# A linear attention with a mixture of experts on one core: the second expert's weights are split in other places, its loads stand behind other rows, and a few small steps around the hand-over change their order

## The chip, the cores and the metric

The kernel runs as one program on one core of a Trainium2 chip. The metric is the device time of the whole program in microseconds (us), as a median of runs; lower is better. The engines are named as in the profile: PE is the matmul engine, DVE the vector engine, ACT the scalar engine, POOL the general-purpose engine, and SP the engine that here only issues transfers (SPq, POOLq and so on are the engines' queues of such instructions). Each engine works through its own instructions in the order in which they were written down, and waits at an instruction until what it needs is there.

## The reference

The inputs are r, k, v, w of shape (4, 8, 768, 48), u (8, 48), a gate (384, 8), and for each of 8 experts w1 (384, 1024) and w2 (1024, 384).

```python
for t in range(S):                                   # attention with a decaying state, per batch and head
    cur = einsum('bhd,bhe->bhde', u * k[t], v[t])
    y[t] = einsum('bhd,bhde->bhe', r[t], state + cur)
    state = w[t][..., None] * state + einsum('bhd,bhe->bhde', k[t], v[t])
x = y as (3072, 384)                                 # 3072 tokens
expert = argmax(x @ w_gate); gate = softmax(x @ w_gate)[expert]
for e in range(8):                                   # each token goes through its one expert
    xe = x[expert == e]
    out[expert == e] = gate * (relu(xe @ w1[e]) @ w2[e])
```

## The kernel before

**First phase.** The attention runs over 24 blocks of 128 tokens; `iteration(n)` issues the stages of several blocks beside each other. After the blocks of a chunk of the sequence are done, a gate decides each token's expert, `rank` (PE) and `place` (DVE) give it a row in that expert's list, and `scatter` (a POOL transfer with computed addresses, line 674) writes the token into `xs` in memory. The last chunk is handled in four groups, `each[0]` to `each[3]`; `chosen(i)` does place, weight and scatter of group i. `gate(...)`, `count(...)` and `act_ex(...)` are the steps ahead of `rank`.

**Second phase.** Every matrix product is done in three matmuls over a high and a low half of each operand (xh, xl; w1h, w1l; w2h, w2l; hh, hl). A weight piece comes from memory (`load_piece`, SP, tiles `wst` and `wsp`) and is split into halves by `split_piece`: ACT writes the high half (line 228), DVE the low one (line 230). An expert has four pieces, i = 0, 1 of w1 and 2, 3 of w2, each split in three parts. There are two sets of split weights, `wts[0]` and `wts[1]`. `stg[e, i]` is the loaded, unsplit piece i of expert e. The eight experts are taken in an order by their number of tokens; the first two are chosen before the attention ends, the other six by `sort_experts` on DVE, followed by `check`.

**Where the phases meet.** The first expert's rows are worked on while the attention ends, in two parts: `pa` (2 x 128 rows) and `pb` (2 x 104 rows). A part loads its rows (`load_rows`, line 248, SP), turns them (`trans`: PE transposes `pt` at line 284, ACT line 285, DVE line 286), and goes through `mm1(f)` for f = 0 to 7 (PE `bank` line 293, then ACT `hh` line 295 and DVE `hl` line 296) and `mm2(q)` (PE `opt` line 310, DVE `ort` line 315, POOL scatter of the result). An `mm2` is 24 matmuls over f = 0 to 7; a dictionary {f: [...]} names what is issued behind its step f. `split_more()` issues the next part of the first expert's own weights. Behind the two parts comes the loop over the other seven experts: `expert(e)` reads the expert's number on SP (line 691), `load_x` its rows, `trans_x` turns them, `feed(e, i)` splits a piece and asks for the next one from memory (`feed(e, i, False)` only asks).

**What sets the order.** Inside `tc.manual_schedule(...)` the engines named there keep the order of the code. SP is not among them, and neither is any engine in the loop over experts: there a scheduler orders, and it may also draw instructions of the loop up between those of the code ahead of it. SP's transfers are issued one after the other, so one that waits holds up those behind it. The pool `wpb` with the second weight set takes the memory of pools that are closed just ahead of it (among them `sm`), so the first writer into the second set waits for the last reader of the tiles that lay there.

Of the kernel before, what the change touches and what calls it, by code (L numbers as in the profile page):

```python
# [8 lines left out]
F32 = mybir.dt.float32  # L9
# [46 lines left out]
def rwkv_moe_kernel(ctx, tc, rkw, vv, ub, wgp, wg, w1, w2, wc, out):  # L56
# [536 lines left out]
            ch["pi", c, b + i] = pi[:, i:i + 1]  # L593

    def sort_keys(k, out):
        ks = sm.tile([1, E], F32, name="ks", tag="ks")
        nc.vector.max(out=ks, in_=k)
        ki = sm.tile([1, E], I32, name="ki", tag="ki")
        nc.vector.tensor_copy(ki, ks)
        nc.vector.tensor_single_scalar(out=out, in_=ki, scalar=E - 1, op=ALU.bitwise_and)  # L600
        return ks
# [15 lines left out]

    def sort_experts():
        cn = counts()
        ch["all"] = sm.tile([1, 1], F32, name="all", tag="all", bufs=1)  # L620
        nc.vector.tensor_reduce(out=ch["all"], in_=cn[0:1, :], axis=AX.X, op=ALU.add)
        c0 = sm.tile([1, NST, E], F32, name="c0", tag="c0", bufs=1)
        nc.vector.tensor_tensor(out=c0, in0=cn[0:1, :].unsqueeze(1).broadcast_to([1, NST, E]), in1=first_e, op=ALU.mult)
        ch["c0"] = sm.tile([1, NST], F32, name="c1", tag="c1", bufs=1)
        nc.vector.tensor_reduce(out=ch["c0"], in_=c0, axis=AX.X, op=ALU.add)
        for i in range(NST):
            nc.vector.scalar_tensor_tensor(out=key, in0=first_e[:, i, :], scalar=-65536.0, in1=key, op0=ALU.mult, op1=ALU.add)
        ch["ks"] = sort_keys(key, order)
# [30 lines left out]
        nc.vector.tensor_copy(flag, lo[:, 4:5])  # L659

    def check():
        bad = sm.tile([1, E + 2 + NST], F32, name="bad", tag="bad", bufs=1)
        nc.vector.tensor_single_scalar(out=bad[:, E:E + 1], in_=ch["all"], scalar=float(NTOK), op=ALU.not_equal)
        nc.vector.tensor_tensor(out=bad[:, 0:E], in0=ch["ks"], in1=capk, op=ALU.is_ge)
        nc.vector.tensor_tensor(out=bad[:, E + 2:E + 2 + NST], in0=ch["c0"], in1=capc, op=ALU.is_gt)
        lo = sm.tile([1, E], F32, name="lo", tag="lo", bufs=1)
        nc.vector.tensor_single_scalar(out=lo[:, 0:E - NST], in_=ch["ks"][:, 0:E - NST], scalar=float(LEAST * E), op=ALU.is_lt)
        nc.vector.tensor_single_scalar(out=lo[:, E - NST:E], in_=ch["c0"], scalar=LEAST - 0.5, op=ALU.is_lt)
        nc.vector.tensor_reduce(out=bad[:, E + 1:E + 2], in_=lo, axis=AX.X, op=ALU.max)
        nc.vector.tensor_reduce(out=any_, in_=bad, axis=AX.X, op=ALU.max)  # L670
# [65 lines left out]
    def iteration(n):  # L736
# [73 lines left out]
        if n == ROUTED:  # L810
# [3 lines left out]
            for i in range(3):  # L814
                wsl.append(wst.tile([P, NT], F32, name="wst", tag="wst"))
                stg[0, i] = load_piece(eid[0], i, wsl[i])
        if n == 19:
            stg[1, 0] = load_piece(eid[1], 0, spare())


    wts = [wt0]
# [124 lines left out]
    with tc.manual_schedule(engines={ET.PE, ET.DVE, ET.Activation, ET.Pool}):  # L946
        for n in range(-3, NB - 2):
            iteration(n)
            if n == 21:
                split_more()  # L950
                stg[1, 2] = load_piece(eid[1], 2, spare())
            if n == 20:
                pa = Part(0, HA // 2, ld.tile([P, NT], F32, name="xg0", tag="rkwt"))
                pa.split_tiles()
                full, banks = banks, banks[0:2]
                stg[1, 1] = load_piece(eid[1], 1, spare())

        lc, n2, n3 = NCH - 1, NB - 2, NB - 1
# [8 lines left out]
        pe_a(n2)  # L967
        dve_at(n2)
        dve_kh(n3)
        stg[1, 3] = load_piece(eid[1], 3, spare())  # L970
        pool_diag(n3)
        act_diag(n3, slice(0, 3))
        pe_lp(n2 - 1)
# [48 lines left out]
        pe_pick(n3)  # L1022
        act_xr(n3)
        rank(each[2])
        chosen(2)
        gate(each[3])
        count(each[3])
        act_ex(each[3])
        split_more()
        pa.mm1(2)  # L1030
        rank(each[3])
        chosen(3)
        split_more()
        pa.mm1(3)
        split_more()
        pa.mm1(4)
        split_more()
        pb = Part(HA, HB // 2, ld.tile([P, NT], F32, name="xg0", tag="rkwt"))
        for f in (5, 6, 7):
            pa.mm1(f)  # L1040
            split_more()
        pb.split_tiles()
        sort_experts()
        expert(2)
        feed(1, 0, False)
        check()
        actx.close()
        wpb = mctx.enter_context(tc.tile_pool(name="wpb", bufs=1))
        wts.append(weight_tiles(wpb))
        split_piece(wts[1], stg[1, 0], 0)  # L1050
        feed(1, 1, False)
        split_piece(wts[1], stg[1, 1], 1)
        feed(1, 2, False)
        load_x(1)
        pa.mm2(0)
        pa.mm2(1, {f: [lambda j=j: pb.trans(j)] for j, f in enumerate((0, 2, 4))})
        banks = full
        nth["b"] = 0
        for f in range(8):
            pb.mm1(f)  # L1060
            if f in (1, 3, 5):
                split_piece(wts[1], stg[1, 2], 2, part=f // 2)
        split_piece(wts[1], stg[1, 3], 3)
        pb.mm2(0, {f: [lambda j=j: trans_x(1, j)] for j, f in enumerate((2, 6))})
        pb.mm2(1, {1: [lambda: trans_x(1, 2)]})
    fin = None
    load_w(0)
    load_w(1)
    for e in range(1, E):
        if e == E - 2:  # L1070
            bad = nc.values_load(flag[0:1, 0:1], min_val=0, max_val=1)
        expert(e + 2)
        if e + 1 < E:
            load_x(e + 1)
        hs = mm1(e, fin)
        fin = mm2(e, hs)
    mctx.close()


# [198 lines left out]
```

## Time and profile before

| what | value |
| --- | --- |
| time, median of 3 runs | 385.31 us (384.91 to 386.27) |
| the profiled execution's own time | 387.93 us |
| its span, first to last instruction | 386.2 us |
| busy: PE, DVE, ACT, POOL | 95%, 71%, 53%, 35% |
| mean granted clock of PE | 0.989 |

The profiled execution has 1.73 us outside its span, and is 0.7% longer than the median. All positions below are us from the start of its span. A row of the timeline gives start, duration, engine, line, operation, output<-input, shapes and count, and in brackets the idle time of the engine just ahead with what ended it. In the rows by windows, each engine's busy time (and count of instructions) comes first, then the granted clock as a share of full speed, the share of time in which the transfer engines were busy, and GB/s.

### The profile page before, as it was taken

How to read it: one execution, taken by the hardware profiler on the slowest of the kernel's cores; microseconds unless marked ns; L12 is line 12 of the kernel's file. 1: busy time of each engine (PE TensorE's matmuls, PEld its weight loads, DVE VectorE, ACT ScalarE, POOL GpSimd, SP SyncE). 2: the span in 40 equal slices, each digit the busy share in tenths (PEclk: the TensorE clock that was granted, in tenths of full speed). 3: DMA queues.
4: the chain of work that ended last, by engine and by line, in shares of the span. 5: the costliest groups of instructions: out<-in, count | busy, mean ns of one | idle time of the engine just before them, and what ended most of it. 6: DMA issues, size and time to landing. Idle time of an engine off the chain costs nothing.

```text
span 386.2 us, 9326 instructions
## 1 busy us (share of the span) xinstructions
PE 368.3 (95%) x3522; PEld 338.5 (88%) x3522; DVE 273.6 (71%) x531; ACT 205.2 (53%) x559; POOL 134.2 (35%) x204
## 2 busy tenths in 40 slices
PE   8989999999999889799999999999999999999991
PEld 6668888888888679799999999999999999999990
DVE  4999999898999868598784792895792853622310
ACT  4989787787777656383625533633633642511200
POOL 4765588868767351102000510400320402112020
PEclk9999999999999999899999999999999999999997
DMA  8999977777518882957394465665365533001010
GB/s 285 406 338 323 308 231 227 241 230 232 164 64 305 272 285 77 282 175 242 114 306 134 145 201 185 193 211 182 98 231 174 157 123 119 21 0 58 1 40 19
DMA packets 32996, 71.44 MB, mean 185 GB/s; under 512 B 3960, under 2 KB 20235, under 8 KB 32946
## 3 DMA queue, kind: packets, MB, share of 16 engines
q1 hardware_dynamic: 29298, 61.32, 49.5%
q0 software_dynamic: 3648, 9.47, 6.8%
q8 instruction: 29, 0.48, 0.5%
q14 instruction: 21, 0.17, 0.1%
HBM read 58.94 MB, written 12.14 MB: 184 GB/s over the span
## 4 chain that ended last, share of the span: by engine, by line
PE 78%; DVE 9%; ACT 5%; issue 3%; DMA 2%; POOL 1%; SPq 1%; POOLq 0%; ACTq 0%; DVEq 0%
PE bank L293 28%; PE bank L920 14%; PE opt L310 13%; PE yp L496 4%; PE ap L484 4%; PE yp L514 3%; PE yq L521 2%; DVE at L383 2%; PE pt L284 2%; DVE pre L361 2%; PE st L505 2%; DMA rkwt<-in_rkw_dram 2%; PE kbank L475 1%; PE op L909 1%; ACT at L355 1%
## 5 line engine op out<-in xcount | busy, mean ns | idle before, releaser
L293 PE MATMUL bank<-xl,w1h 128*128 128x440 f32 (+6 forms) x168 | 58.4, 348 | 0.0
L293 PE MATMUL bank<-xh,w1l 128*128 128x440 f32 (+6 forms) x168 | 58.0, 345 | 0.0
L254 POOL DMA_INDIRECT out_dram<-ot,xg x16 | 21.3, 1332 | 103.2 <-DVE ot L910 99.5
L293 PE MATMUL bank<-xh,w1h 128*128 128x440 f32 (+6 forms) x168 | 55.5, 352 | 0.0
L355 ACT ACTIVATE at<-ident,cl 128x128 f32<-128x128 f32 x168 | 53.8, 393 | 0.0
L254 POOL DMA_INDIRECT out_dram<-ort,xg x13 | 13.0, 1004 | 94.7 <-DVE ort L315 79.6
L295 ACT ACTIVATE hh<-bank 128x256 fp32r<-128x256 f32 (+8 forms) x58 | 26.7, 470 | 34.9 <-PE bank L293 31.2
L230 DVE TENSOR_TENSOR w2l<-wst,w2h 128x512 fp32r<-128x512 f32 x42 | 27.5, 687 | 24.8 <-ACT w2h L228 21.4
L296 DVE SCALAR_TENSOR_TENSOR hl<-bank,hh 128x256 fp32r<-128x256 f32 (+8 forms) x58 | 29.9, 528 | 14.0 <-ACT hh L295 14.0
L334 POOL TENSOR_TENSOR rk<-rkwt 112x512 f32<-112x512 f32 x24 | 30.7, 1280 | 20.4 <-DMA rkwt<-in_rkw_dram 5.1
L383 DVE COPY_PREDICATED at<-cmask,ap 128x512 f32<-128x512 int32 x48 | 32.5, 731 | 2.6 <-PE ap L484 2.5
L343 POOL TENSOR_TENSOR rh<-rkwt,pre 112x512 f32<-112x512 f32 x24 | 28.9, 1205 | 12.0 <-DVE pre L361 10.8
L361 DVE TENSOR_TENSOR_SCAN pre<-rkwt,st 112x533 f32<-112x533 f32 x24 | 30.0, 1250 | 3.6 <-DMA rkwt<-in_rkw_dram 3.6
L293 PEld LDWEIGHTS bank<-xl,w1h 128*128 128x128 f32 x168 | 31.7, 188 | 0.5
L228 ACT ACTIVATE w2h<-wst 128x512 fp32r<-128x512 f32 x42 | 24.5, 626 | 14.2 <-PE bank L920 9.9
L293 PEld LDWEIGHTS bank<-xh,w1l 128*128 128x128 f32 x168 | 31.6, 188 | 0.5
L293 PEld LDWEIGHTS bank<-xh,w1h 128*128 128x128 f32 x168 | 31.4, 188 | 0.5
L369 DVE TENSOR_TENSOR_SCAN suf<-rkwt,st 112x533 f32<-112x533 f32 x24 | 30.3, 1264 | 0.8
L674 POOL DMA_INDIRECT xs<-xr,pi x24 | 25.3, 1053 | 14.0 <-DVE kh L377 3.8
L230 DVE TENSOR_TENSOR w1l<-wst,w1h 128x512 fp32r<-128x512 f32 x42 | 27.5, 685 | 1.0 <-ACT w1h L228 0.8
L310 PE MATMUL opt<-w2h,hh 128*128 128x384 f32 (+3 forms) x82 | 28.2, 350 | 0.0
L310 PE MATMUL opt<-w2h,hl 128*128 128x384 f32 (+3 forms) x82 | 28.0, 343 | 0.0
(164 smaller groups left out, 874.6 us busy)
## 6 DMA issues: line engine op xcount, KB each, us to landing
rkwt<-in_rkw_dram SPq DMA_DIRECT2D x23, 780.0 KB
wst<-in_w_dram SPq DMA_DIRECT2D x42, 256.0 KB
wst<-in_w_dram SPq DMA_DIRECT2D x14, 768.0 KB
vt<-in_vv_dram SPq DMA_DIRECT2D x24, 192.0 KB
wct<-in_wc_dram SPq DMA_DIRECT2D x24, 192.0 KB
xg<-xs SPq DMA_DIRECT2D x5, 579.0 KB
xs<-zrow SPq DMA_DIRECT2D x8, 289.5 KB
wsp<-in_w_dram SPq DMA_DIRECT2D x6, 256.0 KB
```

What stands on the lines that cost most here:

```text
L230: nc.vector.tensor_tensor(out=lo, in0=st[:, cs], in1=hi.bitcast(F32), op=ALU.subtract)
L254: i = nc.gpsimd.indirect_dma_start(out=out[:, :], out_offset=bass.IndirectOffsetOnAxis(ap=t.bitcast(I32)[:, q, DM + 1:DM + 2], axis=0), in ...
L293: nc.tensor.matmul(hp, a, x[:, j, :], start=(i == 0), stop=(i == 8))
L296: nc.vector.scalar_tensor_tensor(out=hl, in0=hp, scalar=0.0, in1=hh.bitcast(F32), op0=ALU.max, op1=ALU.subtract)
L310: nc.tensor.matmul(op, a[:, cs], w2v(wt, w, f), start=(i == 0), stop=(i == 23))
L334: i = nc.gpsimd.tensor_tensor(out=d["rk"], in0=d["r"], in1=d["k"], op=ALU.mult)
L343: nc.gpsimd.tensor_tensor(out=d["rh"], in0=d["r"], in1=d["pre"][:, :, 2:C + 2], op=ALU.mult)
L355: nc.scalar.activation(blk[n]["at"][:, j, q], ident, AF.Copy, scale=blk[n]["ct"][:, 2 * q + j:2 * q + j + 1])
L361: nc.vector.tensor_tensor_scan(out=pre[:, 0:NS], data0=d["w"], data1=floor(n), initial=0.0, op0=ALU.mult, op1=ALU.max)
L369: nc.vector.tensor_tensor_scan(out=suf[:, 0:NS][:, ::-1], data0=d["w"][:, ::-1], data1=floor(n), initial=0.0, op0=ALU.mult, op1=ALU.max)
L383: d["atc"] = nc.vector.copy_predicated(out=d["at"][:, j], mask=cmask.unsqueeze(1).broadcast_to([P, NP_, C]), data=d["ap"][j]).ins
L920: nc.tensor.matmul(pp, w, a, start=(i == 0), stop=(i == 23))
```

## The change

Five things change.

1. The tiles of `sort_keys`, `sort_experts` and `check` are taken from the pool `const` instead of `sm`.
2. The load of the second expert's piece 0, `stg[1, 0]`, is issued behind the rows of `pa` instead of ahead of them. Its piece 3 is issued behind the rows of `pb`, into a buffer that the first expert's piece 1 has left.
3. The gate of the fourth group stands ahead of `chosen(2)`; its `rank` and `chosen(3)` stand behind `pa.mm1(3)` instead of ahead of it.
4. The second expert's splits stood in a block of six between `check` and `pa.mm2(0)`, then three between steps of `pb.mm1`, then three ahead of `pb.mm2`. Now single parts stand at steps of `pa.mm2(0)`, `pa.mm2(1)`, `pb.mm1(1)` to `(6)`, `pb.mm2(0)` and `(1)`. `expert(2)` and the requests for the third expert's pieces stand behind `load_x(1)`, both after `pa.mm2(1)`.
5. The loop over experts is put under `manual_schedule` for POOL alone.

```diff
-        ks = sm.tile([1, E], F32, name="ks", tag="ks")
+        ks = const.tile([1, E], F32, name="ks", tag="ks", bufs=2)
...
-        bad = sm.tile([1, E + 2 + NST], F32, name="bad", tag="bad", bufs=1)
+        bad = const.tile([1, E + 2 + NST], F32, name="bad")
...
-        if n == 19:
-            stg[1, 0] = load_piece(eid[1], 0, spare())
...
                 pa = Part(0, HA // 2, ld.tile([P, NT], F32, name="xg0", tag="rkwt"))
                 pa.split_tiles()
                 full, banks = banks, banks[0:2]
+                stg[1, 0] = load_piece(eid[1], 0, spare())
                 stg[1, 1] = load_piece(eid[1], 1, spare())
...
-        stg[1, 3] = load_piece(eid[1], 3, spare())
...
         rank(each[2])
-        chosen(2)
         gate(each[3])
         count(each[3])
         act_ex(each[3])
+        chosen(2)
         split_more()
         pa.mm1(2)
+        split_more()
+        pa.mm1(3)
         rank(each[3])
         chosen(3)
-        split_more()
-        pa.mm1(3)
         split_more()
         pa.mm1(4)
         split_more()
         pb = Part(HA, HB // 2, ld.tile([P, NT], F32, name="xg0", tag="rkwt"))
+        stg[1, 3] = load_piece(eid[1], 3, wsl[1])
         for f in (5, 6, 7):
             pa.mm1(f)
             split_more()
         pb.split_tiles()
-        sort_experts()
-        expert(2)
-        feed(1, 0, False)
-        check()
         actx.close()
         wpb = mctx.enter_context(tc.tile_pool(name="wpb", bufs=1))
         wts.append(weight_tiles(wpb))
-        split_piece(wts[1], stg[1, 0], 0)
-        feed(1, 1, False)
-        split_piece(wts[1], stg[1, 1], 1)
-        feed(1, 2, False)
-        load_x(1)
-        pa.mm2(0)
-        pa.mm2(1, {f: [lambda j=j: pb.trans(j)] for j, f in enumerate((0, 2, 4))})
+        sort_experts()
+        check()
+
+        def part(i, p):
+            return lambda: split_piece(wts[1], stg[1, i], i, part=p)
+
+        pa.mm2(0, {5: [part(0, 0)]})
+        pa.mm2(1, {0: [lambda: pb.trans(0), part(0, 1)], 2: [lambda: pb.trans(1), part(0, 2)], 4: [lambda: pb.trans(2)]})
+        load_x(1)
+        expert(2)
+        feed(1, 0, False)
+        feed(1, 1, False)
         banks = full
         nth["b"] = 0
         for f in range(8):
             pb.mm1(f)
-            if f in (1, 3, 5):
-                split_piece(wts[1], stg[1, 2], 2, part=f // 2)
-        split_piece(wts[1], stg[1, 3], 3)
-        pb.mm2(0, {f: [lambda j=j: trans_x(1, j)] for j, f in enumerate((2, 6))})
-        pb.mm2(1, {1: [lambda: trans_x(1, 2)]})
+            if 0 < f < 7:
+                part(1 + (f - 1) // 3, (f - 1) % 3)()
+        pb.mm2(0, {0: [part(3, 0)], 2: [lambda: trans_x(1, 0)], 4: [part(3, 1)], 6: [lambda: trans_x(1, 1)]})
+        pb.mm2(1, {1: [lambda: trans_x(1, 2)], 3: [part(3, 2)]})
+        feed(1, 2, False)
...
-    for e in range(1, E):
+    with tc.manual_schedule(engines={ET.Pool}):
+        for e in range(1, E):
```

On DVE, between the sort and the turned rows of `pb`, the kernel before has these instructions in this order (`w1l<-wsp` is a split of the second expert's w1, `x_2835` the turned rows of `pb`, `hhl` and `hl` results of `pb.mm1`):

```order
L670 TENSOR_REDUCE any<-bad 1x1
L230 TENSOR_TENSOR w1l<-wsp,w1h 128x512 x6
L300 TENSOR_SCALAR xg_2357<-xg_2357 128x2
L301 RECIPROCAL xg_2357<-xg_2357 128x2
L315 TENSOR_SCALAR ort<-opt,xg_2357 128x384
L286 TENSOR_TENSOR x_2835<-pt,x_2835 128x208 x3
L315 TENSOR_SCALAR ort<-opt,xg_2357 128x384
L296 SCALAR_TENSOR_TENSOR hhl<-bank,hhl 128x208 x2
```

The changed kernel has there:

```order
L230 TENSOR_TENSOR w1l<-wsp,w1h 128x512
L315 TENSOR_SCALAR ort<-opt,xg_2353 128x384
L286 TENSOR_TENSOR x_2834<-pt,x_2834 128x208
L230 TENSOR_TENSOR w1l<-wsp,w1h 128x512
L286 TENSOR_TENSOR x_2834<-pt,x_2834 128x208
L230 TENSOR_TENSOR w1l<-wsp,w1h 128x512
L286 TENSOR_TENSOR x_2834<-pt,x_2834 128x208
L315 TENSOR_SCALAR ort<-opt,xg_2353 128x384
L296 SCALAR_TENSOR_TENSOR hhl<-bank,hhl 128x208 x2
```

One split instead of six stands ahead of the first turned rows, and one between each two of them; the other three have gone behind the first results of `pb.mm1`. On ACT, in `pb.mm1`, the changed kernel has the following rows, with splits of the third expert's weights (`w1h<-wst`, drawn up from the loop) ahead of the fourth `hh` and of the fifth one:

```order
L295 ACTIVATE hhl<-bank 128x208 x2
L228 ACTIVATE w1h<-wsp 128x512
L295 ACTIVATE hh<-bank 128x208
L228 ACTIVATE w1h<-wsp 128x512
L228 ACTIVATE w1h<-wst 128x512 x2
L295 ACTIVATE hh<-bank 128x208
L228 ACTIVATE w1h<-wsp 128x512
L228 ACTIVATE w1h<-wst 128x512
L295 ACTIVATE hh<-bank 128x208
```

In the kernel before, the three `w1h<-wst` stood together ahead of the fourth `hh` too, so what is new there is mainly when their data are asked for. On SP, around the rows of `pa` (`xg_...<-xs 128x772`), the difference is this piece:

```order
-L211 DMA wsp<-in_w_dram 128x512
-L211 ISA
-L248 DMA xg_2357<-xs 128x772
+L248 ISA
+L248 DMA xg_2353<-xs 128x772
+L211 ISA
+L211 DMA wsp<-in_w_dram 128x512
```

The three loads of `stg[1, 0]` that stood ahead of the rows of `pa` stand behind them. On POOL, at the end of the program, the changed kernel has the load of the flag ahead of the last six scatters, where it stood behind all nine:

```order
L254 DMA out_dram<-ort,xg 3072x384 x3
L1072 TENSOR_LOAD flag
L254 DMA out_dram<-ort,xg 3072x384 x6
L1081 COMPARE_AND_BRANCH
```

The scatters' own order is the same.

## Rows read from the trace of the kernel before

**Rows 1.** The page, busy time by engine: us, share of span, instructions.

```profile
PE 368.3 (95%) x3522; PEld 338.5 (88%) x3522; DVE 273.6 (71%) x531; ACT 205.2 (53%) x559; POOL 134.2 (35%) x204
```

**Rows 2.** Waits of PE, 122 to 182: total us, times, longest.

```profile
PE pt L284 <- DVE x L286: 2.1, 1, 2.1
PE rank L575 <- ACT ex L537: 1.4, 1, 1.4
PE pt L284 <- DVE kh L377: 1.1, 1, 1.1
```

**Rows 3.** Busy times by windows, the last stretch being the loop over experts.

```profile
158.00:162.00 4.00, 2.88 (x11) 2.88 (x12) 1.61 (x5) 0.80 (x3) 0.97 (x1) 0.69 0.86 274
162.00:166.00 4.00, 4.00 (x33) 4.00 (x33) 1.70 (x4) 1.49 (x5) 0.97 (x1) 0.88 1.01 314
166.00:182.00 16.00, 16.00 (x113) 15.54 (x112) 14.27 (x31) 10.34 (x23) 1.09 (x2) 1.00 0.63 189
182.00:372.00 190.00, 189.44 (x1079) 184.86 (x1079) 114.02 (x229) 74.15 (x149) 29.16 (x24) 1.00 0.43 137
```

**Rows 4.** Timeline of PE, from `pa.mm2(0)` to the start of `pb.mm2`.

```profile
149.53 0.44 PE L310 MATMUL opt<-w2h,hh 128*128 128x384 f32 x1
...
156.66 0.34 PE L310 MATMUL opt<-w2l,hh 128*128 128x384 f32 x1
159.12 0.40 PE L284 MATMUL pt<-ident,xg 104*128 104x104 f32 x2 [2.13 <-DVE x L286]
...
162.11 0.59 PE L293 MATMUL bank<-x,w1h 128*128 128x208 f32 x2
...
170.54 0.51 PE L310 MATMUL opt<-w2h,hhl 128*104 128x384 f32 x2
```

**Rows 5.** Timeline of DVE, 142 to 159.

```profile
142.39 0.42 DVE L296 SCALAR_TENSOR_TENSOR hl<-bank,hh 128x256 fp32r<-128x256 f32 x1 [1.12 <-ACT hh L295]
...
144.28 0.69 DVE L230 TENSOR_TENSOR w1l<-wst,w1h 128x512 fp32r<-128x512 f32 x1 [0.45 <-ACT w1h L228]
...
149.06 0.42 DVE L296 SCALAR_TENSOR_TENSOR hl<-bank,hh 128x256 fp32r<-128x256 f32 x1
...
154.07 3.70 DVE L230 TENSOR_TENSOR w1l<-wsp,w1h 128x512 fp32r<-128x512 f32 x6 [0.82 <-ACT w1h L228]
...
158.70 0.65 DVE L286 TENSOR_TENSOR x<-pt,x 128x208 fp32r<-128x208 f32 x2
```

**Rows 6.** Timeline of ACT, the six splits behind the sort.

```profile
153.41 3.24 ACT L228 ACTIVATE w1h<-wsp 128x512 fp32r<-128x512 f32 x6 [2.86 <-DVE any L670]
```

**Rows 7.** Timeline of SP's queue, issues of the loads.

```profile
118.96 2.03 SPq L211 DMA_DIRECT2D wsp<-in_w_dram  x3
127.42 0.33 SPq L248 DMA_DIRECT2D xg<-xs  x1
...
149.74 0.89 SPq L248 DMA_DIRECT2D xg<-xs  x2
153.54 3.62 SPq L211 DMA_DIRECT2D wst<-in_w_dram  x6
...
158.40 0.91 SPq L248 DMA_DIRECT2D xg<-xs  x2
```

**Rows 8.** Timeline of POOL, two of the scatters into `xs`.

```profile
120.27 1.04 POOL L674 DMA_INDIRECT xs<-xr,pi  x1 [0.18 <-issue]
...
146.42 0.97 POOL L674 DMA_INDIRECT xs<-xr,pi  x1 [1.96 <-ACT w2h L228]
```

**Rows 9.** Transfers from 100 to 182: count, median us from issue to landing.

```profile
xs<-xr,pi POOLq DMA_INDIRECT x12, 4.8
```

**Rows 10.** Timeline of all engines from 130 to 132, where `pa`'s rows arrive.

```profile
130.63 0.20 PEld L284 LDWEIGHTS pt<-ident,xg 128*128 128x128 f32 x2 [1.29 <-DMA xg<-xs]
...
131.58 0.42 DVE L286 TENSOR_TENSOR x<-pt,x 128x256 fp32r<-128x256 f32 x1 [0.94 <-ACT x L285]
```

**Rows 11.** Line 1071, the flag's load on POOL: ns, start us.

```profile
L1071 POOLq TENSOR_LOAD <-flag x1: 502/502/502, 378.5 to 378.5; - x1
```

More of the change, by code (lines that the diff above doesn't have):

```diff
@@ L595, in sort_keys @@
     def sort_keys(k, out):
-        ks = sm.tile([1, E], F32, name="ks", tag="ks")
+        ks = const.tile([1, E], F32, name="ks", tag="ks", bufs=2)
         nc.vector.max(out=ks, in_=k)
-        ki = sm.tile([1, E], I32, name="ki", tag="ki")
+        ki = const.tile([1, E], I32, name="ki", tag="ki", bufs=2)
         nc.vector.tensor_copy(ki, ks)
@@ L619, in sort_experts @@
         cn = counts()
-        ch["all"] = sm.tile([1, 1], F32, name="all", tag="all", bufs=1)
+        ch["all"] = const.tile([1, 1], F32, name="all")
         nc.vector.tensor_reduce(out=ch["all"], in_=cn[0:1, :], axis=AX.X, op=ALU.add)
-        c0 = sm.tile([1, NST, E], F32, name="c0", tag="c0", bufs=1)
+        c0 = const.tile([1, NST, E], F32, name="c0")
         nc.vector.tensor_tensor(out=c0, in0=cn[0:1, :].unsqueeze(1).broadcast_to([1, NST, E]), in1=first_e, op=ALU.mult)
-        ch["c0"] = sm.tile([1, NST], F32, name="c1", tag="c1", bufs=1)
+        ch["c0"] = const.tile([1, NST], F32, name="c1")
         nc.vector.tensor_reduce(out=ch["c0"], in_=c0, axis=AX.X, op=ALU.add)
@@ L665, in check @@
         nc.vector.tensor_tensor(out=bad[:, E + 2:E + 2 + NST], in0=ch["c0"], in1=capc, op=ALU.is_gt)
-        lo = sm.tile([1, E], F32, name="lo", tag="lo", bufs=1)
+        lo = const.tile([1, E], F32, name="few")
         nc.vector.tensor_single_scalar(out=lo[:, 0:E - NST], in_=ch["ks"][:, 0:E - NST], scalar=float(LEAST * E), op=ALU.is_lt)
@@ L1068, in rwkv_moe_kernel @@
     load_w(1)
-    for e in range(1, E):
[L1070 to L1076, printed above, removed]
+    with tc.manual_schedule(engines={ET.Pool}):
+        for e in range(1, E):
+            if e == E - 2:
+                bad = nc.values_load(flag[0:1, 0:1], min_val=0, max_val=1)
+            expert(e + 2)
+            if e + 1 < E:
+                load_x(e + 1)
+            hs = mm1(e, fin)
+            fin = mm2(e, hs)
     mctx.close()
```

## The prediction

> **What bounds the kernel now.** I read the page first: PE is busy for 368.3 of 386.2 us [rows 1], so what can be won lies in some 18 us in which PE is idle and in stretches at a low clock. The windows say where not to look: in the loop over experts PE works 189.44 of 190.00 us [rows 3], so nothing won there, and whatever is won before it is carried to the end. The list of PE's waits between 122 and 182 then names three places, all at the hand-over that the change touches: 2.1 us at a transpose `pt` for DVE, 1.4 at `rank`, 1.1 at the first `pt` [rows 2]. Last I read the timelines of the engines behind each wait.
>
> The largest: `pa.mm2(0)` starts at 149.53 and runs evenly to 156.83; then PE waits 2.13 us for the third transpose of `pb`'s rows [rows 4], whose bank DVE has not yet read, because DVE does six splits of the second expert first (154.07 to 157.77) and reaches the first turned rows at 158.70 [rows 5]. The six splits in turn began only at 153.41 on ACT, which waited 2.86 us for the last instruction of the sort, the reader of the memory in which the second weight set lies [rows 6]. Behind PE's wait the granted clock is down: a mean of 0.69 in 158 to 162 (with the wait in it) and 0.88 in 162 to 166 [rows 3], so part of that time is spent at 1.2 in place of 2.4 GHz.
>
> **The change, part by part.**
>
> *Splits out of the block (edits 1 and 4).* On DVE, one split instead of six now stands ahead of the first turned rows, and none waits for the sort's last reader. From 149.53 to 156.83 PE does 39 matmuls (24 of `mm2(0)`, 15 of `mm2(1)`) and two transposes in 7.30 us. With about 0.173 for a matmul (a start every 7.30/41 at most, the transposes a little more), the 9 matmuls and one transpose that are left need 1.84. They took 162.11 - 156.83 = 5.28 [rows 4]. Gain: 3.44, of which 2.13 is the wait and the rest slow clock. `pb.mm1` took 170.54 - 162.11 = 8.43 [rows 4]; its first four us at a clock of 0.88 [rows 3] hold 3.5 us of work at full clock, so 0.4 more comes back. Together **3.85**. The bound above is 4.0; below it is nothing, if the wait only moves.
>
> Where do the splits go? The five that left the block cost DVE 5 x 0.62 = 3.1 us (3.70/6 each [rows 5]). From 158 to 166 DVE is busy 1.61 + 1.70 of 8 us [rows 3], so 4.7 are free there, and PE needs DVE once in 1 us of `pb.mm1`. They are hidden with 1.6 us to spare. In 166 to 182 DVE is full already (14.27 of 16 [rows 3]), but what stood there before (parts of pieces 2 and 3) moves by a few places at equal work; I cost that at nothing, under PE's `pb.mm2` of some ten us. Uncovered, a split costs 0.62. The last split of piece 3 now stands in `pb.mm2(1)`, and the buffer that it frees is awaited by a w1 piece of a later expert, whose load moves back with it by some us; the cover is the second expert's `mm1`, in the stretch in which PE waits for nothing [rows 3], and if it fails the price is that of the third expert's loads below.
>
> *The fourth gate ahead of the third placement (edit 3).* PE's 1.4 us at `rank` go [rows 2]. But `mm2(0)` cannot start before DVE has emptied the bank of `pa.mm1(6)`: that `hl` ends at 149.48, `mm2(0)` starts at 149.53 [rows 4, 5]. From 142.39 to there DVE is busy nearly without a break; its one idle time is 0.45 ahead of a `w1l` [rows 5]. Its work is the same after the change, so it can win 0.45 at most, and the gain lies between 0 and 1.4. I take **0.35**: DVE, not PE, is what `mm2(0)` waits for.
>
> The price: `chosen(3)` stands behind one split and one `hl` more, 0.6 + 0.42 - 0.35, so the last scatter goes out some 0.65 later than 146.42 [rows 8], and with it `pb`'s rows, which wait for it: 149.74 becomes 150.4 [rows 7]. The rows of `pa` were needed 3.2 us after their issue (127.42 to 130.63, where PE's weight load had waited for them [rows 7, 10]); at that, `pb`'s land at 153.6. The first `pt` comes behind 27 matmuls of `mm2`, 149.2 + 4.7 = 153.9. The margin is 0.3 us: I cost it at nothing, and 1.2 if the scatter takes its median of 4.8 to land [rows 9] instead of the 3.3 between its issue and that of the rows (146.42 to 149.74).
>
> *`pa`'s rows ahead of the loads (edit 2).* `pa`'s rows went out at 127.42, 7.15 us after the last scatter they need, issued at 120.27, with 768 KB of `stg[1, 0]` issued in the meantime (118.96 on) [rows 7, 8]. PE's weight load waited 1.29 for the rows, and DVE sat idle 0.94 ahead of their split [rows 10]. DVE is the bound of that stretch, so the gain lies between 0 and 0.94. If the scatter landed in its median 4.8 [rows 9], the rows would go out near 125.3 and be there at 128.5, ahead of the 129.34 at which PE began to wait. I take **0.8**.
>
> Here a page speaks against the change. In the rows, the scatter took 7.15 with the loads in flight against a median of 4.8. The Trainium skill, "DMA: Bandwidth & Descriptors", section "Queues, rings and completion order", says that each transfer engine takes turns between the queues that have work, a packet at a time; a scatter on POOL's queue would then not stand behind SP's loads whole, and taking 768 KB away would bring it little. By that the term would be near 0 and the sum 0.8 less. This case's trace has a slow scatter beside loads, not one without them, so no run here decides it yet.
>
> *The third expert's weights asked for later (edit 4).* Before, their six w1 loads went out from 153.54 [rows 7]. Now they stand behind `load_x(1)`, which waits for a staging buffer until DVE's third split (piece 0) is done, behind the second transpose: near 157.1. Two row issues (0.91) and six loads at 0.60 (3.62/6) follow [rows 7], so the second load leaves near 159.2. Ahead of it and with it go 679 KB of rows and 512 KB of weights: 1.19 MB at 314 GB/s [rows 3] is 3.8 us, and `pa`'s 395 KB, 1.26 us at that rate, took 3.2 in all, so some 1.95 comes on top: landed near 163.7, from 163.6 to 164.4. ACT and DVE take their instructions in order, and two splits of these loads stand ahead of `hh(3)` and `hl(3)`, 1.6 us for both. `pb.mm1(7)` needs the bank that `hl(3)` empties at 158.3 + 7 x 1.007 = 165.35 (8.06 for eight steps). Stall: 163.6 + 1.6 - 165.35 is below 0, 164.4 gives 0.65. I take **-0.3**, from 0 to -0.7.
>
> *The flag's load on POOL (edit 5).* 0.50 us stood behind the last scatter at 378.5 [rows 11]; now it stands ahead of six scatters. POOL still has to wait for that scatter to land, so the gain is 0 to 0.5; I take **0.1**.
>
> *The sum.* 3.85 + 0.35 + 0.8 - 0.3 + 0.1 = 4.8 us. Against the profiled execution: 386.2 + 1.73 outside its span = 387.93, and 383.1 after. That execution is 2.6 us above the median of the runs; the waits are taken to be in all of them, so from 385.31 it is 380.5, and I say **380.6**.
>
> **Rivals.**
>
> 1. *The wait moves to the third expert's loads, and the kernel ends slower.* One mechanism: two splits of `w1h<-wst` stand ahead of `hh(3)`, and PE cannot pass `pb.mm1(7)`. Without that stall the gain is 5.1 us; the stall eats it when the second load lands later than 165.35 + 5.1 - 1.6 = 168.85, 9.6 us after its issue, and 0.3% more at 170. For it speaks that these loads share the engines with 1.4 MB of rows and weights just when the transfer engines are full (1.01 [rows 3]); against it, that nothing in the rows takes 9 us. A milder form, 1 to 3 us late, gives 381.6 to 383.6.
>
> 2. *DVE is the bound and nothing is won in the middle.* If the displaced 3.1 us of splits hold up `hl` in `pb.mm1`, the 3.85 shrinks to 0.75 and the sum to 1.7: 383.6. If PE also waits at the new places for ACT and DVE in order, nothing is left: 385. Against it, the 4.7 us free in 158 to 166.
>
> 3. *`pb`'s rows come late.* The last scatter's 0.65 exceeds the margin of 0.3; with a landing of 4.8 the wait is 1.2 and a low clock behind it costs as much again: 381.8 to 383.
>
> 4. *`pa`'s rows gain nothing*, since the scatter lands when it did: 381.4.
>
> **How the numbers follow.** The forecast itself (379.6 to 381.6) gets 0.42; rival 4 alone 0.16; rival 3 0.13; the mild form of rival 1 0.11; rival 2 at 383.6 0.05, at no change 0.06; slower by rival 1 0.07. A difference of 0.3%, 1.16 us, is about what can be told from no change: faster than 384.15 holds 0.82 (rival 2 at 383.6 and the upper end of the others can fall to either side), within 0.11, slower 0.07. The range from 379.2 (both upper bounds of edits 2 and 3) to 383.8 leaves out the cases of no change and slower, and a little below.
>
> **What would show it.** In the changed profile: no wait of PE at `pt` for DVE, and 9.1 instead of 12.6 us from the first `opt` to `pb.mm1`, with a granted clock of 1.00 through both. PE's wait at `rank` gone, but `mm2(0)` no more than 0.5 earlier against the end of `pa`'s rows. `pa`'s rows out before 126. A wait of PE in `pb.mm1` at steps 6 or 7, with ACT's `w1h` released by a transfer ahead of it, would be the third expert's loads; a PEld wait for `xg` at the first `pt` of `pb`, the late scatter. A transfer that lands later than reckoned is what would make the forecast wrong: the margins for `pb`'s rows and the third expert's loads are under 1 us, all others larger.

## The result and the profile after

The changed kernel takes 381.2 us (four runs, 380.31 to 381.72) against 385.78 us for the kernel before, measured beside it (384.91 to 386.27): a ratio of 0.9883 with a 95% interval from 0.9858 to 0.9908, or 3.5 to 5.5 us less. The profiled execution took 381.39 us with a span of 379.7, 6.5 less than that of before, where the median fell by 4.6; where the other 2 us come from is a main part of what follows.

PE's waits between 122 and 182 (us in total, times, longest):

```profile
PE lp L461 <- ACT ytb L402: 0.2, 1, 0.2
PE bank L293 <- DVE hl L296: 0.2, 1, 0.2
```

All three waits of [rows 2] are gone; one of 0.2 is new, in `pb.mm1`. The windows over the same stretches as in [rows 3], with the same columns:

```profile
158.00:162.00 4.00, 4.00 (x38) 4.00 (x37) 2.23 (x6) 2.42 (x6) 0.31 (x1) 1.00 1.00 270
162.00:166.00 4.00, 3.81 (x30) 3.59 (x30) 4.00 (x9) 4.00 (x11) 0.00 (x0) 1.00 0.67 225
166.00:182.00 16.00, 16.00 (x93) 15.16 (x92) 13.92 (x31) 8.51 (x18) 2.19 (x2) 1.00 0.91 275
182.00:372.00 190.00, 189.29 (x1082) 184.81 (x1080) 111.60 (x222) 72.22 (x146) 29.36 (x24) 1.00 0.42 135
```

The granted clock is 1.00 in all four of these windows (the mean of 0.991 over the whole span has its low stretch early in the attention, 0.79 from 12 to 20 us); the loop over experts is as full as it was. PE's timeline at the places of [rows 4]: the first `opt`, the third transpose, the start of `pb.mm1`, its one wait, the start of `pb.mm2`.

```profile
147.14 0.44 PE L310 MATMUL opt<-w2h,hh 128*128 128x384 f32 x1
...
154.47 0.34 PE L284 MATMUL pt<-ident,xg 104*128 104x104 f32 x2
...
156.25 0.37 PE L293 MATMUL bank<-x,w1h 128*128 128x208 f32 x2
...
163.62 0.48 PE L293 MATMUL bank<-x,w1h 128*128 128x208 f32 x2 [0.19 <-DVE hl L296]
...
164.71 0.51 PE L310 MATMUL opt<-w2h,hhl 128*104 128x384 f32 x2
```

From the first `opt` to `pb.mm1` it is 9.11 us where it was 12.58. `pb.mm1` still takes 8.46: what the clock gave back went into a new stall. Its cause stands in ACT's timeline:

```profile
148.28 0.64 ACT L228 ACTIVATE w1h<-wsp 128x512 fp32r<-128x512 f32 x1 [0.18 <-ACT w2h L228]
...
161.31 1.24 ACT L228 ACTIVATE w1h<-wst 128x512 fp32r<-128x512 f32 x2 [1.00 <-DMA wst<-in_w_dram]
162.46 0.33 ACT L295 ACTIVATE hh<-bank 128x208 fp32r<-128x208 f32 x1
```

The second expert's first split no longer waits for the check (148.28 against 153.41 [rows 6]), but ACT waits 1.00 us for the third expert's weights, with the fourth `hh` behind them in its order. DVE's timeline, of which [rows 5] shows the answering rows:

```profile
140.43 0.42 DVE L296 SCALAR_TENSOR_TENSOR hl<-bank,hh 128x256 fp32r<-128x256 f32 x1 [0.30 <-ACT hh L295]
...
146.67 0.42 DVE L296 SCALAR_TENSOR_TENSOR hl<-bank,hh 128x256 fp32r<-128x256 f32 x1
...
151.38 0.69 DVE L230 TENSOR_TENSOR w1l<-wsp,w1h 128x512 fp32r<-128x512 f32 x1 [0.30 <-DMA xg<-xs]
...
152.72 0.37 DVE L286 TENSOR_TENSOR x<-pt,x 128x208 fp32r<-128x208 f32 x1
```

One split stands between the sort and the first turned rows. `mm2(0)` begins 0.05 after the end of `hl(6)` (146.67 + 0.42), as before. Last, the transfers, POOL first, then SP's queue:

```profile
120.38 1.05 POOL L674 DMA_INDIRECT xs<-xr,pi  x1 [0.18 <-issue]
```

```profile
126.57 0.34 SPq L248 DMA_DIRECT2D xg<-xs  x1
...
148.30 0.89 SPq L248 DMA_DIRECT2D xg<-xs  x2
...
155.21 0.86 SPq L248 DMA_DIRECT2D xg<-xs  x2
157.10 3.38 SPq L211 DMA_DIRECT2D wst<-in_w_dram  x6
```

`pa`'s rows go out 6.2 us after the scatter in place of 7.15; the third expert's weights at 157.10 in place of 153.54.

The ledger below measures both kernels by the same landmarks, each entry a difference of starts in one profile: DVE's last `kh` (line 377), its first turned rows of `pa`, `hl(1)`, the first `opt`, the start of `pb.mm1` and of `pb.mm2`, the last scatter. The second and third columns are two more profiles of the kernel before, the last another of the changed one (told below).

| stretch, us | before | before, 2nd | before, 3rd | changed | changed, 2nd |
| --- | --- | --- | --- | --- | --- |
| start to `kh` | 129.97 | 129.85 | 129.45 | 130.06 | 130.72 |
| `kh` to turned rows of `pa` | 1.61 | 1.40 | 1.25 | 0.60 | 0.59 |
| to `hl(1)` | 10.81 | 9.76 | 10.80 | 9.77 | 11.28 |
| to first `opt` | 7.14 | 7.13 | 7.14 | 6.71 | 6.70 |
| to `pb.mm1` | 12.58 | 11.42 | 12.35 | 9.11 | 9.11 |
| `pb.mm1` | 8.43 | 8.03 | 8.68 | 8.46 | 8.97 |
| to last scatter | 208.20 | 208.22 | 208.19 | 208.07 | 208.03 |
| to the end | 7.46 | 7.49 | 7.44 | 6.92 | 7.10 |
| span | 386.2 | 383.3 | 385.3 | 379.7 | 382.5 |

### The profile page after: what moved, and what is told of

Same layout as the page of the kernel before. It is cut to its first block, busy times and chain, and to the rows that moved or that the text cites. A ratio compares the mean times of both kernels' runs of the same rounds, so it can differ in the third digit from the quotient of the medians.

```text
span 379.7 us, 9324 instructions
## 1 busy us (share of the span) xinstructions
PE 366.3 (96%) x3521; PEld 337.4 (89%) x3522; DVE 274.8 (72%) x531; ACT 205.3 (54%) x559; POOL 135.1 (36%) x204
## 5 line engine op out<-in xcount | busy, mean ns | idle before, releaser
L230 DVE TENSOR_TENSOR w2l<-wst,w2h 128x512 fp32r<-128x512 f32 x45 | 29.4, 686 | 24.0 <-ACT w2h L228 20.9
L228 ACT ACTIVATE w2h<-wst 128x512 fp32r<-128x512 f32 x45 | 26.3, 627 | 14.8 <-PE bank L918 9.9
L484 PE MATMUL ap<-rh,kh 64*128 64x128 f32 (+1 forms) x384 | 27.9, 285 | 0.0
```

What stands on the lines that cost most here:

```text
L230: nc.vector.tensor_tensor(out=lo, in0=st[:, cs], in1=hi.bitcast(F32), op=ALU.subtract)
L484: nc.tensor.matmul(d["ap"][j][:, q, :], d["kh"][rs, q, :], d["rh"][rs, q, :], start=True, stop=True)
```

## The experiments

The runs came in sets, each on one chip with the kernel before beside it. The first set holds the second profile of before and the undoing of edit 2's first half, edit 3 and edit 5; the next one edit 1 undone, edit 1 alone, the block of splits and twice the loads; the next one the last pair; the third profile of before stands alone. Times of different sets are not compared with each other, since the kernel before takes 385.07 us in the first of them, 387.58 and 386.82 in the next two. Ratios to the kernel before in the same set are.

**The kernel before, profiled twice more.** No edit.

> The kernel before, profiled a second time, with nothing changed. In its first profile the ACT instruction hh of pa.mm1(1) began at 141.97, some 1.1 us after the last of its nine matmuls, and this accounts for about 1 us of the difference between the two profiles that no edit explains. Theory: that was a chance event of that one execution; here ACT begins within 0.3 us of the end of the matmuls, as it does in the changed kernel, and the time is near 385.5. Rival: it belongs to the kernel before, is seen here again with some 1 us of idle time ahead of that hh, and is part of what the change won.

It took 385.0 with a span of 383.3. Waits of PE and windows behind the longest:

```profile
PE pt L284 <- DVE x L286: 2.1, 1, 2.1
PE pt L284 <- DMA xg<-xs: 0.9, 1, 0.9
PE rank L575 <- ACT ex L537: 0.3, 1, 0.3
```

```profile
156.00:158.00 2.00, 0.27 (x3) 0.27 (x4) 1.81 (x6) 0.58 (x2) 0.33 (x1) 1.00 0.88 307
158.00:160.00 2.00, 2.00 (x16) 2.00 (x14) 0.61 (x2) 0.35 (x1) 0.64 (x1) 1.00 0.70 211
```

The theory held, and more was off than it said: ACT began at once (9.76 to `hl(1)` in place of 10.81), PE's wait at `rank` was 0.3 and not 1.35, and behind the same 2.1 us of waiting the clock stayed at 1.00, so that the stretch from `opt` to `pb.mm1` was 1.16 shorter and `pb.mm1` 0.40. That left open which of the two executions is the odd one.

> The kernel before, profiled a third time, unaltered. Its first profile had two things that its second had not: hl(1) 3.3 us behind hl(0) in place of 2.3, and a granted clock of 0.5 behind PE's wait of 2.1 us, which cost some 1.2 us to the start of pb.mm1 and 0.4 in it. Theory (the low clock behind that wait comes in some executions and not in others): from the first opt to pb.mm1 either 11.4 us (clock 1.00 behind the wait) or 12.6 (0.5), and a time near 385 or near 387 with it. Rival (it belongs to the wait, and the second profile was the odd one): 12.6.

It took 387.05, and is like the first:

```profile
156.00:158.00 2.00, 0.11 (x1) 0.00 (x0) 1.86 (x6) 0.58 (x2) 0.00 (x0) 1.00 0.99 305
158.00:160.00 2.00, 1.77 (x8) 1.77 (x9) 0.83 (x3) 0.35 (x1) 0.97 (x1) 0.74 0.84 300
160.00:162.00 2.00, 2.00 (x9) 2.00 (x9) 0.62 (x1) 0.00 (x0) 0.00 (x0) 0.50 1.10 351
```

So there are two kinds of execution of the same kernel: in two of three the late `hl(1)` and the low clock behind the wait came together, in one neither came. The wait of 2.1 is in all three.

How often each kind came among the timed runs can be read from their mean granted clock. In the thirteen profiles told here it is 0.984 to 0.991 in the seven that have a stretch at a low clock while PE still works, and 0.992 to 0.996 in the six that have none. The runs of the kernel before have 0.993 or more in all 11 of the first set, 0.991 or less in 21 of 23 of the second and in 8 of 11 of the third. Its kind thus goes with the set and its chip: where the median is 385.07 no run shows the low clock, where it is 387.58 or 386.82 most do.

**The load ahead of `pa`'s rows again** (edit 2, first half).

```diff
+        if n == 19:
+            stg[1, 0] = load_piece(eid[1], 0, spare())
...
-                stg[1, 0] = load_piece(eid[1], 0, spare())
```

> The changed kernel with one step of edit 2 undone: the 768 KB of the second expert's piece 0 are asked for ahead of pa's rows again. Theory (the rows wait for the last scatter, and the scatter lands later when more load bytes are ahead of it): rows issued some 0.9 us later, 7.1 us after the scatter in place of 6.2, PE and DVE wait about 1 us at the first turned rows, and the time is 0.9 us above the changed kernel, near 382.1. Rival (turns between queues packet by packet, the loads cost the scatter little): gap between scatter and rows stays at 6.2 us and the time at 381.2.

381.67 us, ratio 0.9918 (0.9904 to 0.9931). From the scatter (118.93) to the rows' issue (125.45) it was 6.5, PE's weight load waited for the rows again, and the turned rows came 1.06 behind `kh` in place of 0.60:

```profile
128.78 0.20 PEld L284 LDWEIGHTS pt<-ident,xg 128*128 128x128 f32 x2 [0.78 <-DMA xg<-xs]
```

Half of the theory's 0.9 in this one execution; over this and the two kernels' first profiles the step is worth 0.46 to 1.0.

**Twice the loads ahead of `pa`'s rows.** As above, with `stg[1, 1]` too.

> The changed kernel with 1.5 MB of loads ahead of pa's rows: both w1 pieces of the second expert, twice what the kernel before had there. Theory (bytes ahead of the last scatter delay its landing): from the scatter to the issue of the rows 7.5 to 8 us, against 6.0 to 6.2 with none and 6.5 to 7.15 with 768 KB; turned rows of pa 0.8 us later still, and 382.5 to 383. Rival (turns packet by packet, the scatter stands beside the loads and not behind them): the gap stays under 7.2, as with 768 KB.

386.98 us, ratio 0.9986 (0.996 to 1.0012): about 4 us of the change's gain are lost. But not where the theory had it. The scatter and the wait for the rows:

```profile
119.66 1.05 POOL L674 DMA_INDIRECT xs<-xr,pi  x1 [0.18 <-issue]
```

```profile
131.96 0.29 PEld L284 LDWEIGHTS pt<-ident,xg 128*128 128x128 f32 x2 [3.22 <-DMA xg<-xs]
```

The rows were issued at 126.36, 6.7 us behind the scatter, no later than with half the bytes: the rival was right about the scatter. The rows themselves then took 5.6 us to arrive (126.36 to 131.96), against 3.05 in the changed kernel (126.57 to 129.62) and 3.2 before [rows 7, 10]. They are on SP's own queue, behind the loads. The later rows are 3.1 of the 4 us (first turned rows 3.74 behind `kh` in place of 0.60). More went behind the wait, where PE ran at half clock from 132 to 138:

```profile
134.00:136.00 2.00, 2.00 (x20) 1.64 (x18) 0.86 (x3) 1.16 (x3) 0.55 (x1) 0.50 0.26 99
```

**The fourth gate behind the third placement again** (edit 3).

```diff
         rank(each[2])
+        chosen(2)
         gate(each[3])
         count(each[3])
         act_ex(each[3])
-        chosen(2)
         split_more()
         pa.mm1(2)
-        split_more()
-        pa.mm1(3)
         rank(each[3])
         chosen(3)
+        split_more()
+        pa.mm1(3)
```

> The changed kernel with edit 3 undone: third placement ahead of the fourth gate, fourth rank and placement ahead of pa.mm1(3). Theory (DVE is what pa.mm2(0) waits for, so PE's own wait is worth little): PE waits about 1.3 us at rank again, but mm2(0) starts only some 0.4 us later relative to pa's rows, and the time is 0.4 above the changed kernel, 381.6. Rival (PE is what counts there): 1.3 us more, 382.5.

381.6 us, ratio 0.9911 (0.9897 to 0.9924). From `hl(1)` (140.35) to the first `opt` (147.47) it was 7.12 against 6.71: 0.41 lost, as the theory had it. PE waited 0.3 at `rank`, not the expected 1.3; the 1.35 of [rows 2] belonged to the executions with a late `hl(1)`.

**The loop without the manual order for POOL** (edit 5).

```diff
-    with tc.manual_schedule(engines={ET.Pool}):
-        for e in range(1, E):
+    for e in range(1, E):
```

> The changed kernel with edit 5 undone: the loop over experts is not under a manual order for POOL. Theory: POOL's load of the flag (0.5 us) is behind the last scatter again and the stretch from the last scatter to the end of the span grows from 6.9 to 7.4 us, so the time is 0.5 above the changed kernel, 381.7. Rival (the landing of the last scatter covers it, as the prediction had it): 0.1 us or nothing.

381.32 us, ratio 0.9911 (0.9895 to 0.9928). The flag's load on POOL, here and in the changed kernel:

```profile
L1071 POOLq TENSOR_LOAD <-flag x1: 508/508/508, 371.8 to 371.8; - x1
```

```profile
L1072 POOLq TENSOR_LOAD <-flag x1: 507/507/507, 324.3 to 324.3; - x1
```

The load at 371.8 is the one behind the last scatter: it begins when the result that this scatter waits for is done (371.73), and the scatter's own recorded start is 372.00. From there to the end of the span (379.5) it was 7.5 against 6.92. The theory's 0.5 is there in the profile; the times, 0.1 apart and from two sets, can't tell it. All thirteen profiles agree on the sign: 7.44 to 7.50 in the five with the load behind the last scatter, 6.89 to 7.14 in the eight with the load ahead of the last six.

The changed kernel was not run in this set. The ratios of the three versions with one edit undone (0.991 to 0.992) lie 0.003 above its 0.9883, over 1 us, which is more than the 0.4 to 0.6 that each profile shows; but the intervals touch or overlap, and in this set no run of the kernel before shows the low clock that the change can take away.

**The sort's tiles back in the old pool** (edit 1).

```diff
-        bad = const.tile([1, E + 2 + NST], F32, name="bad")
+        bad = sm.tile([1, E + 2 + NST], F32, name="bad", tag="bad", bufs=1)
...
-        actx.close()
-        wpb = mctx.enter_context(tc.tile_pool(name="wpb", bufs=1))
-        wts.append(weight_tiles(wpb))
         sort_experts()
         check()
+        actx.close()
+        wpb = mctx.enter_context(tc.tile_pool(name="wpb", bufs=1))
+        wts.append(weight_tiles(wpb))
```

> The changed kernel with edit 1 undone: the sort's and the check's small tiles lie in the pool whose memory the second weight set takes over, so the first split again waits for the last instruction of the check. Theory (with only one split ahead of the first turned rows, nobody waits for it): ACT's first split begins near 150.8 in place of 148.3 and is done before DVE is free for its low half; PE waits nowhere new and the time stays within 0.2 of 381.2. Rival (that wait of 2.9 us was the thing to remove): PE waits at the turned rows of pb again, 1 to 2 us, 382.2 to 383.3.

382.65 us, ratio 0.9867 (0.9813 to 0.992) to a kernel before of 387.58: no worse than the whole change. ACT's first split began only behind the check again (`any` at 152.24, the split at 152.63; the profile puts the end of this wait down to a transfer of rows), and DVE sat idle 0.63 ahead of its low half. But from the first `opt` (148.94) to `pb.mm1` (158.03) it was 9.09, with no wait at the transposes. Once single splits are spread out, the wait for the check costs nothing that this profile or the ratio shows.

**Edit 1 alone, on the kernel before.**

> The kernel before with edit 1 alone. Theory (DVE does the sort and then six splits in order, so ACT's 2.9 us of waiting are worth only the 0.82 us that DVE sat idle ahead of the first low half): ACT's splits run during the sort, DVE's six splits begin 0.8 earlier, PE's wait for the third transpose falls from 2.1 to 1.3, and the time from 385.1 to 384.3. Rival A (the whole 2.9 us of ACT's wait come forward): the wait of PE is gone, 382.9. Rival B (nothing): 385.1.

386.02 us, ratio 0.9951 (0.9926 to 0.9977): 0.9 to 2.9 us faster, more than the theory's 0.8. PE's wait:

```profile
160.98 0.40 PE L284 MATMUL pt<-ident,xg 104*128 104x104 f32 x2 [1.59 <-DVE x L286]
```

The wait fell by 0.5, but `opt` to `pb.mm1` is 10.91 (151.90 to 162.81) and `pb.mm1` 8.02, against 12.35 and 8.68 in the third profile of before, which was of the same kind (`hl(1)` 3.3 behind `hl(0)`): behind the shorter wait the clock is 1.00 in 160 to 164. That accounts for 2.1 us. Whether the edit kept the clock up is likely and not shown: the second profile of before has 1.00 behind a wait of 2.1. Of the timed runs, 4 of 12 have a mean clock of 0.991 or less, against 21 of 23 of the kernel before in this set. The profiled execution is itself 2.2 us above its median: PE waited 1.8 for `pa`'s rows and the clock fell behind that wait:

```profile
134.00:136.00 2.00, 2.00 (x16) 1.44 (x16) 1.45 (x3) 0.61 (x3) 1.04 (x2) 0.55 0.81 260
```

**The block of six splits back** (main part of edit 4, the rest of the change kept).

```diff
+        split_piece(wts[1], stg[1, 0], 0)
+        split_piece(wts[1], stg[1, 1], 1)
-        pa.mm2(0, {5: [part(0, 0)]})
-        pa.mm2(1, {0: [lambda: pb.trans(0), part(0, 1)], 2: [lambda: pb.trans(1), part(0, 2)], 4: [lambda: pb.trans(2)]})
+        pa.mm2(0)
+        pa.mm2(1, {f: [lambda j=j: pb.trans(j)] for j, f in enumerate((0, 2, 4))})
...
-            if 0 < f < 7:
-                part(1 + (f - 1) // 3, (f - 1) % 3)()
+            if f in (1, 3, 5):
+                part(2, f // 2)()
```

> The changed kernel with the main part of edit 4 undone: the six splits stand in one block between check and pa.mm2(0) again, the next three between steps 1, 3 and 5 of pb.mm1; the rest of the change stays. Theory (the block on DVE is what PE waited for, less the 0.8 that edit 1 saves): PE waits 1.3 us at the third transpose, 10.4 us from the first opt to pb.mm1 in place of 9.1, at full clock; the stall in pb.mm1 (0.4) goes, since the rows of the second expert and the third expert's loads are asked for earlier. Time 382.1. Rival (the low clock of the first profile belongs to that wait too): 1.3 to 1.7 more, 383.5 to 383.8.

383.59 us, ratio 0.9898 (0.9858 to 0.9938). PE waited as the theory had it, at a clock of 1.00:

```profile
PE pt L284 <- DVE x L286: 1.3, 1, 1.3
```

From `opt` to `pb.mm1` it was 10.65 (149.57 to 160.22), 1.54 above the changed kernel, and `pb.mm1` took 8.02, 0.44 below: 1.1 net in the profile. By the ratios it is 0.6 against the whole change, with an interval that does not tell it from 0; beside it in the same set, the version with edit 1 undone, in which the block is spread, takes 0.9 less (382.65).

**The third expert's weights asked for first, and the changed kernel beside it.**

```diff
+        expert(2)
+        feed(1, 0, False)
+        feed(1, 1, False)
         pa.mm2(0, {5: [part(0, 0)]})
...
         load_x(1)
-        expert(2)
-        feed(1, 0, False)
-        feed(1, 1, False)
```

> The changed kernel with one move: the third expert's number and the requests for its two w1 pieces stand ahead of pa.mm2(0), and so ahead of load_x(1) on SP's queue, in place of behind it. Theory (the 0.4 us that pb.mm1 takes above 8.03 is the wait for those loads): they are asked for near 150.5 in place of 157.1 and land before ACT comes to them; ACT's 1.0 us of waiting for the transfer in pb.mm1 is gone, pb.mm1 takes 8.0 to 8.2 in place of 8.46, and the time is 0.3 to 0.4 below the changed kernel on the same chip, a ratio to the kernel before some 0.001 lower. Rival A (the scheduler draws three splits in place of two ahead of hh(3), so hl(3) is as late as before): pb.mm1 stays at 8.4 and the time the same. Rival B (the rows of pb or of the second expert come later behind these loads): a wait of PE at pt, 0.5 to 1 us slower.

> The changed kernel once more, with nothing altered, on the chip of the run before it in this list, so that the two stand side by side. In some profiles of both kernels, hl(1) of pa follows hl(0) by 3.3 us or more, in others by 2.3. Theory (it goes with the chip or the execution, not with the kernel): this profile has one of the two values, and the other kernel of this call has the same one; ratio to the kernel before near 0.988. Rival (the change removed it): 2.3 here, whatever the other kernel shows.

382.27 us against 383.24 for the changed kernel beside it; ratios 0.9863 (0.9827 to 0.9898) and 0.9884 (0.9852 to 0.9917). In the second profile of the changed kernel ACT waited 1.3 us for the weights and PE 0.7 in `pb.mm1` (and, with the late `hl(1)`, 0.4 at `rank` and 0.8 at the first `opt`):

```profile
PE bank L293 <- DVE hl L296: 0.7, 1, 0.7
```

With the loads asked for at 152.5 `pb.mm1` takes 8.03 (157.90 to 165.93) and neither wait is there. ACT had three splits of those weights ahead of the fourth `hh`, as rival A had it (161.86 to 163.42), but their data were there and nothing was late. PE waited 0.4 for `pa`'s rows, which were issued at 127.27, ahead of anything that the move touches; at `pb`'s transposes it did not wait, so rival B did not come. The version that asks first has the lowest ratio measured here, though the one with edit 1 undone is as low within its interval (0.9867); the intervals of the two ratios overlap, so the 1.0 us between the medians is likely and not certain, and the mechanism is shown by the profiles. Both profiles have the late `hl(1)` (3.3 and 3.8 behind `hl(0)`), so the change did not remove that.

## Why the prediction was right, and where not

Forecast 380.6, measured 381.2, within the range and on the side that was given 0.82. The mechanisms were the ones named; two of the five terms had the wrong size, in opposite directions, and that the total came so near is in part luck: the terms as measured add up to 3.8 against the profile of before without a low clock (below), 1.0 short of the forecast's 4.8. The 4.6 of the medians (3.5 to 5.5) lies between the 3.6 of that pair of spans and the 6.5 of the first pair.

*Splits out of the block, 3.85.* The wait went and the stretch runs in 9.11, within 0.03 of the 9.14 (7.30 + 1.84) worked out. The gain was mis-sized for the runs that are timed: it is 3.24 to 3.47 against the two executions with a low clock, and 2.31 against the one without (11.42 to 9.11), in which `pb.mm1` had no slow clock to give back either. The step that failed is "the waits are taken to be in all of them": the wait was, the low clock behind it was not. Its 1.2 + 0.4 us, and the 1.05 of the late `hl(1)`, add up to the 2.6 us by which the profiled execution of before lay above the median of its runs, a number that stood in the prediction itself. For that set the median was the better base; in the sets at 387.58 and 386.82 the low clock is in most runs and more of the 3.85 would be there to win. Edit 1 and edit 4 overlap: edit 1 alone was worth 1.9 (0.9 to 2.9) in a set in which most runs of before have the low clock, edit 4 undone lost 0.6 to 1.1, and with edit 4 made, edit 1 adds nothing that shows.

*Fourth gate, 0.35.* Measured 0.42 and, undone, 0.41. DVE, not PE, was the limit. The delay came as reckoned, the last scatter 4.63 behind `hl(1)` in place of 4.03, but the price did not come due: it went out at 145.06 and the rows of `pb` at 148.30, 3.2 later, and PE did not wait for them.

*`pa`'s rows, 0.8.* Measured 0.65 to 1.0 from `kh` to the turned rows, 0.46 in the undone version. The way there was wrong in part: the scatter did not land in 4.8 but in 6.2, and the rows went out at 126.57, not before 126. This was enough, because they were needed at 129.6. In the version that asks first they went out 6.65 behind the scatter with no load ahead, and the turned rows came 0.94 behind `kh`, so part of the difference is chance of one execution.

The prediction gave a rule of the Trainium skill ("DMA: Bandwidth & Descriptors", "Queues, rings and completion order"), that a transfer engine takes turns between the queues a packet at a time, by which this term would be near nothing. The runs agree with it in one point: from the scatter's issue to that of the rows, which wait for its landing, it is 6.5 to 8.0 us in the five profiles with 768 KB of these loads ahead and 6.7 in the one with 1.5 MB, so twice the bytes do not make it later. The conclusion drawn from it does not hold: in the seven profiles without these loads it is 6.0 to 6.7, and the means, 7.1 and 6.2, are 0.9 apart. With 768 KB the term lies in this gap, since the rows themselves then take 3.1 to 3.3 us from issue to PE's weight load, and 3.0 to 3.1 without the loads where that weight load waited for them. With 1.5 MB it lies in the rows' own 5.6 us; how a scatter on another queue comes to land 0.9 later beside 768 KB is open.

*The third expert's loads, -0.3.* Measured -0.43 (8.46 against 8.03), and -0.9 in the second profile. The place was right to the step: ACT's `w1h` released by a transfer, `hl(3)` late, PE waiting in `pb.mm1`. Asked for first, all of it comes back. Rival 1 was thus on the path in its mildest form.

*The flag's load, 0.1.* Measured 0.57 and, undone, 0.58 (over all profiles 0.3 to 0.6); this term was mis-sized. The reason given for the low value, that POOL must wait for the last scatter to land anyway, does not cover it. A likely way is that the branch waits for the load and POOL's closing steps stand behind the branch; no run parts it from others. The last scatter is 5.96 us earlier than in the first profile of before (378.74 to 372.78), and the closing drain 6.5 (380.7 to 374.2).

Terms as measured against the second profile of before: 0.80 - 0.01 + 0.42 + 2.31 - 0.43 + 0.15 + 0.57 = 3.8, less 0.2 by which the attention ended later in that execution, is the 3.6 between the spans 383.3 and 379.7. A sum over two single executions is no finer than that: `kh` alone comes anywhere from 128.61 to 131.05 in the thirteen profiles.

## What to carry to other kernels

A profile that is longer than the median of the timed runs has something in it that the median run has not: before its rows are added up into a gain, a second profile of the unchanged kernel, on another chip too, shows which of its waits and clocks repeat. Behind a wait on an in-order engine, look for the block of work that nobody needs yet and spread it, and then ask what the same engine will meet first in its new order: here the next transfer, asked for 3.6 us later, took back 0.4. Small rows that are needed soon should be issued ahead of large loads on the same queue: here 768 KB ahead went with a scatter that landed some 0.9 later, and 1.5 MB held up the rows themselves by 2.5.

## What was not expected of the hardware

The same kernel has two kinds of execution. Of the thirteen profiles told here, eight (two of before, one of the changed kernel, five of the variants) have `hl(1)` 3.3 to 3.8 us behind `hl(0)`, and five (one of before, one of the changed kernel, three of the variants) have 2.3, with the same instructions. In the late ones ACT begins `hh(1)` 1.3 to 1.9 us after the recorded start of the last matmul that it waits for, in the others 0.3. As far as the chip is on record it goes with it: all four profiles of one chip are early, all seven of three others late, with kernels of both kinds among them. Why is open, since no row between shows what ACT waits for.

Behind a wait of 2.1 us, with PE at full work before it, the granted clock fell to 0.50 (1.2 GHz) in two of three executions and stayed at 1.00 in the third; behind waits of 1.3 and 1.6 in two variants it stayed at 1.00. The length of the wait alone does not decide it: behind the 3.0 and the 1.8 for `pa`'s rows (twice the loads, edit 1 alone) it fell, and three profiles, both of the changed kernel among them, have 0.74 to 0.83 over 8 us of the attention, where PE waited no longer than 0.8 at a time. What decides it is open. The low clock and the late `hl(1)` came together in the kernel before, but two variants (edit 1 undone, the weights asked for first) have the late `hl(1)` and no low clock while PE works.
